# Linear-attention block on one core: the last two token tiles of each slab of keys and values interleaved in two PSUM banks

## The chip, the cores and the metric

The kernel runs on one core of a Trainium2 chip. The metric is the device time of one execution in microseconds (us). Beside the timed runs there is one profiled execution, from which every row below comes; its own time differs a little from that of the timed runs.

## What is computed

One block for 2048 tokens of width 1024, in fp32: layer norm, a linear attention with 32 heads of 32 and a learned feature map, an output projection and residual, and a second layer norm with an MLP of width 3584 and residual.

```python
q, k, v = split(layernorm(x) @ wqkv)            # 32 heads of 32
pk = einsum("bhsd,hdf->bhsf", k, w_phi)         # the same for q
phi_k = concat([softmax(pk), softmax(-pk)])     # 64 features a head
kv = einsum("bhsf,bhsd->bhfd", phi_k, v)        # sums over all tokens
z  = einsum("bhsf->bhf", phi_k)
o  = (phi_q @ kv) / (phi_q @ z + 1e-6)
h  = x + o @ wo
out = h + relu(layernorm(h) @ w1) @ w2
```

## The kernel before

**Work and its order.** The 2048 tokens are 16 tiles of 128. They are worked on in two halves, hf = 0 (tiles 0 to 7) and hf = 1 (tiles 8 to 15). In each half come four slabs of keys and values, s = 0 to 3 (8 heads each: 256 columns of keys, with w_phi folded in, and 256 of values), then two slabs of queries. "Slab (1,2)" below is hf = 1, s = 2. Within a slab the tiles follow each other. Every engine works through its instructions strictly in the order in which the program issues them, and that order is written by hand: TensorE's work is a list of items (`item`), each of 8 steps, and other work is hung on steps of that list (`when(step, ...)`, `do(item, k, ...)`).

**Products.** A product in fp32 is made of three fast ones: each operand is split into a high and a low part, and a step issues high x high, high x low and low x high (L204, L205, L206), each 128 x 512 columns. A tile of a slab takes 8 steps, one for each weight unit k = 0 to 7, and adds up in one PSUM bank named `mm` (four banks in turn). Tile 0 (or 8), the first of a slab, uses `sum3` (L195, L196, L199), where the product with the low half of a unit comes three steps late.

**Weight units.** A unit is 128 x 512 of weights. A DMA brings it into a ring of six raw tiles; ScalarE copies the high half (L126), and VectorE or GpSimd subtracts for the low half (L130) into a ring of ten places (`RW = 10`). A place falls free after the last step that uses its unit, and then the next unit is split (`Units.advance`). The eight units of a slab are used by all its eight tiles, so two places hold units of the next slab ahead, and the other six are split as the old ones fall free.

**Softmax of a key tile.** `kv_first` runs at the end of the tile's last step: ScalarE copies the values out (L452), VectorE takes maximum and minimum and subtracts them (L455, L456, L458, L459). Then the schedule hangs three stages on the steps behind item n of the tile: the exponential on ScalarE (`kv_exp`, L463), sums, reciprocal and product to phi on VectorE (`kv_second`, L468, L469, L471, tile `kphi`), and the sum z on GpSimd (`kv_z`, L479). For each group of four tiles `kv_third` then issues 64 short matmuls on TensorE, 16 a tile, from phi and the values (L490):

```python
for (hf, s, t), n in kv_n.items():
    when(8 * n + 11, kv_exp, (hf, s, t))
    when(8 * n + 13, kv_second, (hf, s, t))
    when(8 * n + 18, kv_z, (hf, s, t))
    when(8 * (n + (3 - t % 4)) + 22, kv_third, (hf, s, t))
```

For a query tile `q_first` (L550, L551, L555, L556) stands in the place of `kv_first`.

**Other work at the same time.** In the second half GpSimd also multiplies exponentials of queries by z, 128 x 1024 (`xl`, L614), VectorE reduces them (`xtz`, L618), GpSimd makes the denominators (`qden`, L652, L653) and VectorE their reciprocals (`smx`, L622). GpSimd further makes sums of MLP weights (L388, tiles `b` and `xn`).

Of the kernel before, what the change touches and what calls it, by code (L numbers as in the profile page):

```python
# [23 lines left out]
HT = NT // 2  # L24
# [117 lines left out]
def kernel(  # L142
# [22 lines left out]
    def mm_bank():  # L165
        return psum.tile([P, 512], F32, name="mm", bufs=4)
# [15 lines left out]
    def woven(ap):  # L182

        return ap.rearrange("p (a b) -> p b a", a=2)

    def unwoven(ps):

        return ps.rearrange("p (b a) -> p a b", a=2)
# [13 lines left out]
    def mm3(ps, a_hi, a_lo, b_hi, b_lo, first, last, more=False):  # L202
        b_hi, b_lo = woven(b_hi), woven(b_lo)
        pe.matmul(ps, a_hi, b_hi, start=first, stop=False, skip_group_check=more)  # L204
        pe.matmul(ps, a_hi, b_lo, start=False, stop=False, skip_group_check=more)  # L205
        pe.matmul(ps, a_lo, b_hi, start=False, stop=last, skip_group_check=more)  # L206
# [4 lines left out]
    def do(n, k, f, *args):  # L211
        at[n, k].append((f, args))
# [232 lines left out]
    xT = {}  # L445
    e_of, v_of, phi_of, kv_ps, kd_of = {}, {}, {}, {}, {}

    def kv_first(key, ps):

        pk = ps.rearrange("p (h f a) -> p a h f", a=2, f=32)[:, 0]  # L450
        vt = kp.tile([P, 256], F32, name="vt", bufs=6)
        act.activation(vt, unwoven(ps)[:, 1], AF.Copy)  # L452
        v_of[key] = vt
        m = kp.tile([P, 2, 8], F32, name="kmx", bufs=2)
        v.tensor_reduce(out=m[:, 0, :], in_=pk, op=ALU.max, axis=AX.X)  # L455
        v.tensor_reduce(out=m[:, 1, :], in_=pk, op=ALU.min, axis=AX.X)  # L456
        e = kp.tile([P, 8, 2, 32], F32, name="ke", bufs=2)
        v.tensor_sub(e[:, :, 0, :], pk, m[:, 0, :, None].to_broadcast([P, 8, 32]))  # L458
        v.tensor_sub(e[:, :, 1, :], m[:, 1, :, None].to_broadcast([P, 8, 32]), pk)  # L459
        e_of[key] = e  # L460
# [62 lines left out]
    def project(t, keys):  # L523
        ps = mm_bank()
        if t in (HT, 0) and keys[0] != ("kv", 0, 0, 0):
            def part(k):
                w = W.get(keys[k])
                return xT[t][:, 0, k, :], xT[t][:, 1, k, :], w[:, 0, :], w[:, 1, :]
            yield from sum3(ps, [partial(part, k) for k in range(NK)], 3)
            return ps  # L530
        for k in range(NK):
            w = W.get(keys[k])
            mm3(ps, xT[t][:, 0, k, :], xT[t][:, 1, k, :], w[:, 0, :], w[:, 1, :], k == 0, k == NK - 1)
            yield
        return ps

    def kv_item(key, keys):
        ps = yield from project(key[2], keys)
        kv_first(key, ps)

    def q_item(s, t, keys):
        ps = yield from project(t, keys)
        q_first(s, t, ps)

    def q_first(s, t, ps):

        pq = ps.rearrange("p (h f w) -> p w h f", w=2, f=32)
        pa = ps.rearrange("p (a c f w) -> p w a c f", w=2, a=2, c=4)
        m = pqp.tile([P, 2, 16], F32, name="qmx", bufs=2)
        v.tensor_reduce(out=m[:, 0, :].rearrange("p (w h) -> p w h", w=2), in_=pq, op=ALU.max, axis=AX.X)  # L550
        v.tensor_reduce(out=m[:, 1, :].rearrange("p (w h) -> p w h", w=2), in_=pq, op=ALU.min, axis=AX.X)  # L551
        e = pqp.tile([P, 4, 2, 4, 32], F32, name="qe", bufs=2)
        m = m.rearrange("p s (w a c) -> p s w a c", w=2, a=2)
        x = e.rearrange("p (w a) s c f -> p s w a c f", w=2)
        v.tensor_sub(x[:, 0], pa, m[:, 0, :, :, :, None].to_broadcast([P, 2, 2, 4, 32]))  # L555
        v.tensor_sub(x[:, 1], m[:, 1, :, :, :, None].to_broadcast([P, 2, 2, 4, 32]), pa)  # L556
        e_of[s, t] = e
# [434 lines left out]
    def item(gen, *args, keys):  # L992
        items.append((gen, args + (keys,)))
        steps.extend((k,) for k in keys)
        return len(items) - 1

    kv_n, q_n, wo_n, up_n, down_n = {}, {}, {}, {}, {}
    for hf in range(2):
        for s in range(4):
            for t in range(hf * HT, (hf + 1) * HT):  # L1000
                kv_n[hf, s, t] = item(kv_item, (hf, s, t), keys=[("kv", hf, s, k) for k in range(NK)])
        for s in range(2):
            for t in range(hf * HT, (hf + 1) * HT):
                q_n[s, t] = item(q_item, s, t, keys=[("q", hf, s, k) for k in range(NK)])

    wo_first = len(items)
    for b, tiles in enumerate(groups):
        for hf in range(2):

            pairs = b == 0 and hf == 0  # L1010
            for j in range(0, 4, 2 if pairs else 1):
# [3 lines left out]
                for half in range(2):  # L1015
                    n = item(wo_pair, tiles[j:j + 2], hf, half, keys=[("wo", hf, 4 * half + k // 2) for k in range(8)])
# [8 lines left out]
    for b in range(2):  # L1025
        for m in DOWN:
            for p in range(NP):
                down_n[b, m, p] = len(items)
                keys = ("a", b, m, p), ("w2", b, m, p)
# [13 lines left out]
    def when(step, f, *args):  # L1043

        if step < 8 * first_up:
            do(step // 8, step % 8, f, *args)
        else:
            do(first_up + (step - 8 * first_up) // 4, step % 4, f, *args)
# [5 lines left out]
    for t in range(1, NT):  # L1054
        n = t - 1 if t < HT else q_n[1, t - HT] + 1
# [32 lines left out]


    for (hf, s, t), n in kv_n.items():  # L1090
        when(8 * n + 11, kv_exp, (hf, s, t))
        when(8 * n + 13, kv_second, (hf, s, t))
        when(8 * n + 18, kv_z, (hf, s, t))
        when(8 * (n + (3 - t % 4)) + 22, kv_third, (hf, s, t))
        if hf == 1 and t == NT - 1:
            do(n + 3, 7, z_sum, s)
            do(n + 3, 7, kv_turn, s)
# [75 lines left out]
    for u in range(32):  # L1173
# [12 lines left out]
        if u in EARLY:  # L1186
            slab, after = EARLY[u]
# [77 lines left out]
    for b in range(2):  # L1265
        for m in DOWN:
            n = down_n[b, m, NP - 1] + 1
# [10 lines left out]
    W = Units(nc, wraw, wring, load, ready, steps)  # L1278
    half = consts.tile([P, 1], F32, name="half")
# [98 lines left out]
```

## Time and profile before

| | |
|---|---|
| time, median of 3 runs | 1791.92 us (1791.12 to 1792.53) |
| profiled execution, its own time | 1796.31 us |
| its span, first to last instruction | 1794.3 us |
| mean granted TensorE clock | 0.996 of full speed |
| busy: TensorE / VectorE / ScalarE / GpSimd | 1771.9 / 1075.9 / 770.1 / 980.2 us |
| matmuls | 10088 |

Busy time is the time in which an engine has an instruction running. A granted clock of 1.00 is the full speed of TensorE, 0.50 half of it.

### The profile page before, as it was taken

What the parts mean: (1) busy time and instruction counts of PE and PEld (TensorE: products, weight loads), DVE (VectorE), ACT (ScalarE), POOL (GpSimd) and SP (SyncE); (2) the same over time, 40 slices, a digit from 0 to 9 for tenths busy, and PEclk for the clock granted to TensorE, in tenths of its full rate; (3) what the DMA queues carried; (4) which work ended last, traced back from release to release, by engine and by line L of the source; (5) the groups of instructions that cost most, each with busy time, mean ns of one, the idle gap of its engine ahead of it and who ended that gap; (6) DMA issues with size and microseconds to landing.
All of it is one profiled execution on the core that took longest, in us unless ns stands there. A gap on an engine that the chain in (4) does not pass through costs nothing.

```text
span 1794.3 us, 28978 instructions
## 1 busy us (share of the span) xinstructions
PE 1771.9 (99%) x10088; PEld 1527.4 (85%) x10088; DVE 1075.9 (60%) x1647; ACT 770.1 (43%) x1379; POOL 980.2 (55%) x991
## 2 busy tenths in 40 slices
PE   9999999999999999999999999999999999999998
PEld 7888888888888877888888888888888888888887
DVE  7888789777789877564766673444434333443333
ACT  5322245233333333355555554444444444444442
POOL 4888755898847987342333224432354544544543
PEclk9999999999999999999999999999999999999999
DMA  6989799665477776887889987777677777877775
GB/s 224 294 289 319 257 286 290 204 191 173 156 226 215 234 228 212 286 266 225 267 267 266 350 286 230 252 248 228 217 245 227 219 240 240 260 227 228 226 227 175
DMA packets 335747, 435.14 MB, mean 243 GB/s; under 512 B 29808, under 2 KB 195696, under 8 KB 335600
## 3 DMA queue, kind: packets, MB, share of 16 engines
q1 hardware_dynamic: 301808, 416.51, 73.3%
q10 hardware_dynamic: 33792, 16.78, 3.3%
q8 instruction: 79, 1.29, 0.3%
q14 instruction: 68, 0.56, 0.1%
HBM read 295.31 MB, written 137.89 MB: 241 GB/s over the span
## 4 chain that ended last, share of the span: by engine, by line
PE 78%; POOL 9%; DVE 5%; DMA 4%; issue 2%; ACT 1%; SPq 0%; ACTq 0%; POOLq 0%; DVEq 0%
PE mm L204 18%; PE mm L205 18%; PE mm L206 18%; PE ac L206 4%; PE ac L204 4%; PE ac L205 4%; PE tp L204 2%; PE tp L206 2%; PE tp L205 2%; POOL b L388 2%; POOL w L130 2%; POOL xl L614 1%; PE mm L199 1%; PE mm L195 1%; POOL zacc L479 1%
## 5 line engine op out<-in xcount | busy, mean ns | idle before, releaser
L130 POOL TENSOR_TENSOR w<-raw,w 128x512 fp32r<-128x512 f32 x357 | 475.5, 1334 | 626.1 <-ACT w L126 599.9
L126 ACT ACTIVATE w<-raw 128x512 fp32r<-128x512 f32 x686 | 410.3, 625 | 468.4 <-PE mm L206 200.7
L130 DVE TENSOR_TENSOR w<-raw,w 128x512 fp32r<-128x512 f32 x329 | 274.3, 835 | 467.4 <-ACT w L126 456.5
L204 PE MATMUL mm<-w,xT 128*128 128x512 f32 x680 | 262.2, 386 | 0.0
L205 PE MATMUL mm<-w,xT 128*128 128x512 f32 x680 | 257.9, 379 | 0.6 <-POOL w L426 0.6
L206 PE MATMUL mm<-w,xT 128*128 128x512 f32 x680 | 257.8, 379 | 0.0
L204 PE MATMUL mm<-hT,w 128*128 128x512 f32 x624 | 236.5, 379 | 0.0
L205 PE MATMUL mm<-hT,w 128*128 128x512 f32 x624 | 236.5, 379 | 0.0
L206 PE MATMUL mm<-hT,w 128*128 128x512 f32 x624 | 236.5, 379 | 0.0
L388 POOL TENSOR_TENSOR b<-b 128x256 f32<-128x256 f32 x164 | 133.8, 816 | 52.2 <-DMA b<-in_w_dram 41.1
L204 PE MATMUL mm<-w 128*128 128x512 f32 x392 | 148.6, 379 | 0.0
L205 PE MATMUL mm<-w 128*128 128x512 f32 x392 | 148.6, 379 | 0.0
L206 PE MATMUL mm<-w 128*128 128x512 f32 x392 | 148.6, 379 | 0.0
L204 PEld LDWEIGHTS mm<-w,xT 128*128 128x128 f32 x680 | 128.5, 189 | 21.6 <-issue 3.3
L206 PEld LDWEIGHTS mm<-w,xT 128*128 128x128 f32 x680 | 128.5, 189 | 18.4 <-DVE xT L180 0.3
L205 PEld LDWEIGHTS mm<-w,xT 128*128 128x128 f32 x680 | 128.6, 189 | 18.1 <-POOL w L426 1.2
L204 PEld LDWEIGHTS mm<-hT,w 128*128 128x128 f32 x624 | 117.9, 189 | 16.8
L206 PEld LDWEIGHTS mm<-hT,w 128*128 128x128 f32 x624 | 117.9, 189 | 16.7
L205 PEld LDWEIGHTS mm<-hT,w 128*128 128x128 f32 x624 | 117.9, 189 | 16.7
L463 ACT ACTIVATE ke<-ke 128x512 f32<-128x512 f32 x64 | 40.3, 629 | 105.4 <-DVE ke L459 105.3
L205 PEld LDWEIGHTS mm<-w 128*128 128x128 f32 x392 | 74.1, 189 | 10.5
L206 PEld LDWEIGHTS mm<-w 128*128 128x128 f32 x392 | 74.1, 189 | 10.5
(192 smaller groups left out, 3359.8 us busy)
## 6 DMA issues: line engine op xcount, KB each, us to landing
raw<-t SPq DMA_DIRECT2D x224, 256.0 KB, 4.0
raw<-ad SPq DMA_DIRECT2D x196, 256.0 KB, 3.1
raw<-in_w_dram SPq DMA_DIRECT2D x168, 256.0 KB, 3.4
ad<-c SPq DMA_DIRECT2D x112, 256.0 KB, 4.0
ad<-s SPq DMA_DIRECT2D x84, 256.0 KB, 4.8
b<-in_w_dram SPq DMA_DIRECT2D x41, 512.0 KB, 6.3
t<-b SPq DMA_DIRECT2D x41, 512.0 KB, 4.7
ed<-qe ACTq DMA_DIRECT2D x64, 256.0 KB, 3.8
```

The source lines that it names most:

```text
L126: nc.scalar.activation(w[:, 0, :], raw[1], AF.Copy)
L130: eng.tensor_tensor(out=w[:, 1, :], in0=raw[1], in1=w[:, 0, :].bitcast(F32), op=ALU.subtract)
L195: pe.matmul(ps, a_hi, woven(b_hi), start=first and k == 0, stop=False, skip_group_check=more)
L199: pe.matmul(ps, a_hi, woven(b_lo), start=False, stop=last and j == n - 1, skip_group_check=more)
L204: pe.matmul(ps, a_hi, b_hi, start=first, stop=False, skip_group_check=more)
L205: pe.matmul(ps, a_hi, b_lo, start=False, stop=False, skip_group_check=more)
L206: pe.matmul(ps, a_lo, b_hi, start=False, stop=last, skip_group_check=more)
L388: pool.tensor_tensor(out=tsum[*u, *out], in0=tsum[*u, *a], in1=tsum[*u, *b], op=ALU.subtract)
L463: act.activation(e_of[key], e_of[key], AF.Exp)
L479: pool.tensor_tensor(out=zacc[s], in0=zacc[s], in1=phi_of[key], op=ALU.add)
L614: pool.tensor_tensor(out=e, in0=e, in1=zb[:, q, None, P * r:P * (r + 1)].to_broadcast([P, 8, P]), op=ALU.mult)
```

## The change

For every slab of keys and values but (0,0), the last two tiles, called A and B here (6 and 7, or 14 and 15), are one pair in two items: in each item four units are used, each for A and then for B, in two banks. The number of items and steps stays the same. `kv_first` of A is issued one step before the pair's end, that of B at its end. Both tiles now count from the second item; the stages of B behind `kv_first` come three steps later than those of A, and `kv_third` stays where it was. Below the new function, lines of the program move down by 17, so L614, L618, L622, L550 are L631, L635, L639, L567 in the changed kernel.

```diff
--- before.py
+++ after.py
@@ -537,6 +537,23 @@
     def kv_item(key, keys):
         ps = yield from project(key[2], keys)
         kv_first(key, ps)
+
+    pair_ps = {}
+
+    def kv_pair(hf, s, tiles, half, keys):
+
+        if half == 0:
+            for t in tiles:
+                pair_ps[t] = mm_bank()
+        for k in range(8):
+            c, t = 4 * half + k // 2, tiles[k % 2]
+            w = W.get(keys[k])
+            mm3(pair_ps[t], xT[t][:, 0, c, :], xT[t][:, 1, c, :], w[:, 0, :], w[:, 1, :], c == 0, c == 7)
+            yield
+            if c == 7 and k < 7:
+                kv_first((hf, s, t), pair_ps.pop(t))
+        if half == 1:
+            kv_first((hf, s, t), pair_ps.pop(t))
 
     def q_item(s, t, keys):
         ps = yield from project(t, keys)
@@ -997,8 +1014,14 @@
     kv_n, q_n, wo_n, up_n, down_n = {}, {}, {}, {}, {}
     for hf in range(2):
         for s in range(4):
-            for t in range(hf * HT, (hf + 1) * HT):
+            last = 0 if hf == s == 0 else 2
+            for t in range(hf * HT, (hf + 1) * HT - last):
                 kv_n[hf, s, t] = item(kv_item, (hf, s, t), keys=[("kv", hf, s, k) for k in range(NK)])
+            if last:
+                two = (hf + 1) * HT - 2, (hf + 1) * HT - 1
+                for half in range(2):
+                    n = item(kv_pair, hf, s, two, half, keys=[("kv", hf, s, 4 * half + k // 2) for k in range(8)])
+                kv_n[hf, s, two[0]] = kv_n[hf, s, two[1]] = n
         for s in range(2):
             for t in range(hf * HT, (hf + 1) * HT):
                 q_n[s, t] = item(q_item, s, t, keys=[("q", hf, s, k) for k in range(NK)])
@@ -1088,10 +1111,11 @@
 
 
     for (hf, s, t), n in kv_n.items():
-        when(8 * n + 11, kv_exp, (hf, s, t))
-        when(8 * n + 13, kv_second, (hf, s, t))
-        when(8 * n + 18, kv_z, (hf, s, t))
-        when(8 * (n + (3 - t % 4)) + 22, kv_third, (hf, s, t))
+        after = 3 if t % HT == HT - 1 and (hf, s) != (0, 0) else 0
+        when(8 * n + after + 11, kv_exp, (hf, s, t))
+        when(8 * n + after + 13, kv_second, (hf, s, t))
+        when(8 * n + after + 18, kv_z, (hf, s, t))
+        when(8 * kv_n[hf, s, t | 3] + 22, kv_third, (hf, s, t))
         if hf == 1 and t == NT - 1:
             do(n + 3, 7, z_sum, s)
             do(n + 3, 7, kv_turn, s)
```

TensorE at the end of slab (1,1), its last six rows before; `w` are units, `xT` the tiles of tokens (3842 is A, 3934 is B), `mm` the banks:

```order
L204 MATMUL mm_4839<-w_4368,xT_3934 128x512
L205 MATMUL mm_4839<-w_4368,xT_3934 128x512
L206 MATMUL mm_4839<-w_4368,xT_3934 128x512
L204 MATMUL mm_4839<-w_4383,xT_3934 128x512
L205 MATMUL mm_4839<-w_4383,xT_3934 128x512
L206 MATMUL mm_4839<-w_4383,xT_3934 128x512
```

The same place after:

```order
L204 MATMUL mm_4785<-w_4365,xT_3842 128x512
L205 MATMUL mm_4785<-w_4365,xT_3842 128x512
L206 MATMUL mm_4785<-w_4365,xT_3842 128x512
L204 MATMUL mm_4786<-w_4365,xT_3934 128x512
L205 MATMUL mm_4786<-w_4365,xT_3934 128x512
L206 MATMUL mm_4786<-w_4365,xT_3934 128x512
```

Two steps used two units, and use one unit now, in two banks.

GpSimd ahead of the end of slab (1,2), before; `zacc` is the sum z, the splits are L130:

```order
L614 TENSOR_TENSOR xl_5252<-xl_5252,zb_2981 128x1024
L388 TENSOR_TENSOR xn_5225<-xn_5225 128x256 x3
L130 TENSOR_TENSOR w_5367<-raw_4869,w_5367 128x512
L388 TENSOR_TENSOR xn_5225<-xn_5225 128x256
L479 TENSOR_TENSOR zacc2_362<-zacc2_362,kphi_5344 128x512
L130 TENSOR_TENSOR w_5387<-raw_4896,w_5387 128x512
L130 TENSOR_TENSOR w_5410<-raw_4964,w_5410 128x512
L652 TENSOR_TENSOR qden_5404<-qden_5404,smx_2984 128x32
```

And after:

```order
L130 TENSOR_TENSOR w_5327<-raw_4857,w_5327 128x512
L479 TENSOR_TENSOR zacc2_362<-zacc2_362,kphi_5266 128x512
L631 TENSOR_TENSOR xl_5252<-xl_5252,zb_2975 128x1024
L388 TENSOR_TENSOR xn_5225<-xn_5225 128x256 x4
L130 TENSOR_TENSOR w_5375<-raw_4878,w_5375 128x512
L479 TENSOR_TENSOR zacc2_362<-zacc2_362,kphi_5350 128x512
L130 TENSOR_TENSOR w_5392<-raw_4930,w_5392 128x512
L669 TENSOR_TENSOR qden_5400<-qden_5400,smx_2978 128x32
```

The first of the three splits has moved ahead of the product `xl`.

VectorE at the end of slab (1,1), before. `ke_4927` belongs to B, `mm_4930` is the bank of T0, the first tile of the next slab:

```order
L618 TENSOR_REDUCE xtz_4946<-xl_4823 128x32
L468 TENSOR_REDUCE ksm_4951<-ke_4927 128x16
L469 RECIPROCAL ksm_4951<-ksm_4951 128x16
L471 TENSOR_TENSOR kphi_4954<-ke_4927,ksm_4951 128x512
L455 TENSOR_REDUCE kmx_4980<-mm_4930 128x8
L456 TENSOR_REDUCE kmx_4980<-mm_4930 128x8
L458 TENSOR_TENSOR ke_4983<-mm_4930,kmx_4980 128x8x32
L459 TENSOR_TENSOR ke_4983<-kmx_4980,mm_4930 128x8x32
```

After, `ke_4907` is A's, `ke_4921` B's and `mm_4924` the bank of T0:

```order
L635 TENSOR_REDUCE xtz_4945<-xl_4836 128x32
L130 TENSOR_TENSOR w_4947<-raw_4830,w_4947 128x512
L468 TENSOR_REDUCE ksm_4956<-ke_4907 128x16
L469 RECIPROCAL ksm_4956<-ksm_4956 128x16
L471 TENSOR_TENSOR kphi_4959<-ke_4907,ksm_4956 128x512
L455 TENSOR_REDUCE kmx_4980<-mm_4924 128x8
L456 TENSOR_REDUCE kmx_4980<-mm_4924 128x8
L458 TENSOR_TENSOR ke_4983<-mm_4924,kmx_4980 128x8x32
L459 TENSOR_TENSOR ke_4983<-kmx_4980,mm_4924 128x8x32
L468 TENSOR_REDUCE ksm_4990<-ke_4921 128x16
L469 RECIPROCAL ksm_4990<-ksm_4990 128x16
L471 TENSOR_TENSOR kphi_4993<-ke_4921,ksm_4990 128x512
```

Where B's three instructions stood, A's stand, behind a split; B's have moved behind the four of T0. At the end of (1,3) it is the same, with the four instructions of the first query tile (L567, L568, L572, L573) between A's and B's, and no split ahead of A's; at the end of (1,2) as at (1,1), with the reciprocal `smx` and no `xtz` ahead of the split.

## Rows read from the trace of the kernel before

**Rows 1.** The page: busy us of the engines, share of the span, instructions.
```profile
PE 1771.9 (99%) x10088; PEld 1527.4 (85%) x10088; DVE 1075.9 (60%) x1647; ACT 770.1 (43%) x1379; POOL 980.2 (55%) x991
```

**Rows 2.** Waits of TensorE: waited for, us in total, times, longest us.
```profile
PE tp L268 <- ACT xin L261: 4.3, 1, 4.3
PE mm L199 <- POOL w L130: 3.7, 5, 1.0
...
PE ac L685 <- DVE qe L672: 2.2, 1, 2.2
```

**Rows 3.** TensorE timeline: start, us, instruction, [idle before, releaser]; behind (1,1), (1,2).
```profile
392.72 0.70 PE L199 MATMUL mm<-w,xT 128*128 128x512 f32 x2 [0.65 <-POOL w L130]
394.39 0.70 PE L199 MATMUL mm<-w,xT 128*128 128x512 f32 x2 [0.97 <-POOL w L130]
...
440.24 0.70 PE L199 MATMUL mm<-w,xT 128*128 128x512 f32 x2 [1.02 <-POOL w L130]
441.46 0.70 PE L199 MATMUL mm<-w,xT 128*128 128x512 f32 x2 [0.52 <-POOL w L130]
```

**Rows 4.** TensorE timeline: L490 behind (1,0), (1,1), (1,2) and (1,3).
```profile
352.57 1.10 PE L490 MATMUL ac<-kphi,vt 128*32 128x64 f32 x64
...
399.56 1.26 PE L490 MATMUL ac<-kphi,vt 128*32 128x64 f32 x64
...
446.63 1.10 PE L490 MATMUL ac<-kphi,vt 128*32 128x64 f32 x64
...
492.51 0.43 PE L490 MATMUL ac<-kphi,vt 128*32 128x64 f32 x16 [0.16 <-DVE kphi L471]
```

**Rows 5.** VectorE timeline, end of slab (1,1).
```profile
397.25 1.22 DVE L618 TENSOR_REDUCE xtz<-xl 128x32 f32<-128x1024 f32 x1 [1.98 <-POOL xl L614]
398.38 0.68 DVE L468 TENSOR_REDUCE ksm<-ke 128x16 f32<-128x512 f32 x1
...
399.38 0.85 DVE L471 TENSOR_TENSOR kphi<-ke,ksm 128x512 f32<-128x512 f32 x1
400.16 0.41 DVE L455 TENSOR_REDUCE kmx<-mm 128x8 f32<-128x256 f32 x1
...
401.48 0.72 DVE L130 TENSOR_TENSOR w<-raw,w 128x512 fp32r<-128x512 f32 x1
```

**Rows 6.** VectorE timeline, end of slab (1,3).
```profile
490.51 0.68 DVE L468 TENSOR_REDUCE ksm<-ke 128x16 f32<-128x512 f32 x1
...
491.50 0.86 DVE L471 TENSOR_TENSOR kphi<-ke,ksm 128x512 f32<-128x512 f32 x1
492.28 0.68 DVE L550 TENSOR_REDUCE qmx<-mm 128x16 f32<-128x512 f32 x1
...
494.67 0.34 DVE L622 RECIPROCAL smx<-qden 128x32 f32<-128x32 f32 x1
```

**Rows 7.** VectorE timeline, end of slab (1,2).
```profile
441.99 0.35 DVE L622 RECIPROCAL smx<-qden 128x32 f32<-128x32 f32 x1 [2.84 <-POOL qden L653]
...
443.20 1.77 DVE L471 TENSOR_TENSOR kphi<-ke,ksm 128x512 f32<-128x512 f32 x1
```

**Rows 8.** GpSimd timeline, end of slab (1,2).
```profile
429.42 2.38 POOL L614 TENSOR_TENSOR xl<-xl,zb 128x1024 f32<-128x1024 f32 x1 [2.33 <-DMA xl<-ed]
...
438.93 2.48 POOL L130 TENSOR_TENSOR w<-raw,w 128x512 fp32r<-128x512 f32 x2
```

**Rows 9.** VectorE timeline, end of slab (1,0).
```profile
349.06 0.41 DVE L455 TENSOR_REDUCE kmx<-mm 128x8 f32<-128x256 f32 x1
```

**Rows 10.** Windows: length, busy us of PE, PEld, DVE, ACT, POOL, PEclk, DMA, GB/s.
```profile
668.00:675.00 7.00, 6.93 (x50) 4.96 (x50) 3.42 (x5) 3.25 (x8) 6.53 (x9) 0.56 0.19 43
701.00:705.00 4.00, 4.00 (x28) 2.97 (x13) 3.34 (x6) 2.61 (x7) 4.00 (x3) 0.57 0.58 195
500.00:520.00 20.00, 20.00 (x94) 17.53 (x93) 16.47 (x25) 6.11 (x8) 4.95 (x8) 1.00 0.74 231
429.40:441.40 12.00, 10.52 (x48) 8.56 (x46) 8.66 (x15) 6.79 (x15) 11.83 (x10) 1.00 0.07 24
```

## The prediction

> **What bounds the kernel now.** I read the waits of TensorE first, then its timeline at each end of a slab, then the timelines of VectorE and GpSimd at the same places, and last the granted clock around the long idles. TensorE is the bound: the page gives it 1771.9 us busy of a span of 1794.3 [rows 1]. So a change can only give back idle time of TensorE, or add some. In the slabs of keys and values there is one kind of idle that this change aims at: the first tile of a slab waits for the low half of a weight unit that GpSimd still has to split, 3.7 us in five waits [rows 2]. They stand behind three of the seven slabs that are paired now: 0.65 and 0.97 us behind slab (1,1), 1.02 and 0.52 us behind (1,2) [rows 3], and the rest of the 3.7, 0.54 us, behind (0,2). That is the most that earlier splits can give back, 0.21% of the time. What can be measured here from no change is about 0.2%, 3.6 us, so even the whole of it would hardly be seen.
>
> The second thing to read is what TensorE takes from VectorE at the same ends: the sums over a group of four tiles (L490) need phi of the slab's last tile, and 64 short matmuls in order stand or fall with the last 16. At the end of (1,1) and (1,3) this phi is ready only as it is wanted. Undelayed, 64 of them take 1.10 us, as behind (1,0) and (1,2); behind (1,1) the row has 1.26, and behind (1,3) the last 16 wait 0.16 us for kphi [rows 4]. In the rows of VectorE the phi of (1,1) ends at 399.38 + 0.85 = 400.23 [rows 5], that of (1,3) at 491.50 + 0.86 = 492.36 [rows 6]. There is no slack there: each us that phi comes later is a us in which TensorE stands.
>
> **The change, part by part.** Matmuls: the same number, with the same operands, in another order. A pair holds two of the four banks named mm at once. The second was last used by a tile whose last matmul lies a whole tile of 24 matmuls back, and VectorE needs it for 1.3 us (four rows such as 400.16 to 401.48 [rows 5]). Cost 0; a bank not drained would show as a wait for L452 or L459 on the first matmuls of a pair.
>
> Units: those of the old slab fall free at every second step of 16 instead of at every step of the last 8, so six splits of the next slab may start up to eight steps earlier. Behind (0,2) and (1,2) GpSimd can use that. Behind (1,2) it idles 2.33 us for a DMA right before L614 at 429.42, and from there to the end of the two splits that TensorE waits for (438.93, 2.48 us) it is busy 11.83 of 12.00 us [rows 8, 10]; the order of after puts one split ahead of that idle, so the two end earlier by one split, half of the 2.48 at least, and of the 1.54 us of waits I let 1.4 go (bounds 1.2 and 1.54). The 0.54 behind (0,2) goes too. Behind (1,1) the same set of GpSimd instructions stands ahead of the last split as before; what is gained or not there doesn't matter, for VectorE is later still (next).
>
> Softmax of the last tiles: this is the costly part. VectorE works in the order written. Before, the three instructions that make the last phi (L468, L469, L471) stood ahead of the softmax start of the next slab's first tile T0. Now A's three stand in that place, then T0's start, and B's three only then, since B's stage comes three steps later. L490 keeps its step.
> At (1,1), up to the reduction that waits for GpSimd's xl the row is as before (397.25, 1.22 us). Then a split stands ahead of A, 0.72 us as the one at 401.48; A's phi ends at 400.23 + 0.72 = 400.95. T0's four instructions take from 400.16 to 401.48, 1.32 us, and B's three as long as the last three before, from 398.38 to 400.16, 1.78 us [rows 5]. So B's phi ends at 400.95 + 1.32 + 1.78 = 404.05 instead of 400.23: 3.8 us later, with no slack before. TensorE coming earlier by a saved wait only waits longer: +3.8 us against before, with no gain. Bounds: 2.5 if contention on VectorE falls, 5 if L471 takes 1.77 us as in [rows 7] instead of 0.85.
> At (1,3) nothing is put ahead of A, which ends at 492.36. Between A and B stand q's four instructions, from 492.28 to 494.67, 2.39 us, and B's three take 490.51 to 492.28, 1.77 us [rows 6]: B's phi comes 4.2 us later, and there was no slack: +4.2 us, bounds 3 to 5.2.
> At (1,2) the last phi ended at 443.20 + 1.77 = 444.97 [rows 7]; L490 started at 446.63, its last quarter some 0.66 us on [rows 4], so phi had 2.3 us. TensorE comes 1.4 us earlier, which leaves 0.9. The new order costs 0.72 + 1.32 + 1.78 = 3.8; the reciprocal ahead of it, late by 2.84 us for GpSimd [rows 7], comes some 1.75 us earlier with GpSimd's work. 3.8 - 1.75 - 0.9 is 1.1; I take +1.0, bounds 0 and 2.
> At the four other ends GpSimd and VectorE have room. The nearest case is (1,0): T0's start was at 349.06 [rows 9], 1.32 + 1.78 behind it is 352.2, and the last quarter of L490 is wanted at 352.57 + 0.66 = 353.2 [rows 4]. Cost 0, with 1.0 us of cover.
>
> What the idles do to TensorE's clock: the kernel before has two long idles further on. An idle of 4.3 us for L261 and one of 2.2 us for L672 [rows 2]. Behind the first, the stretch 668 to 675 has a mean granted clock of 0.56: at half clock most of the time, 1.2 instead of 2.4 GHz, and 7.00 x 0.44 = 3.1 us of work lost. Behind the second, 701 to 705 has 0.57: 4.00 x 0.43 = 1.7 us [rows 10]. The new idles at (1,1) and (1,3), about 4 us each, lie between the two; the one at (1,1) is cut into 0.8 and 3 us by A's 16 short matmuls. I take the middle, 2.4 us each: +4.8, bounds 0 (neither drops) and 6.2 (both as the first). The 1 us at (1,2) is as long as the wait at 440.24, and the stretch with that wait in it has the full clock, 1.00 [rows 3, 10]: 0.
> The Trainium skill, TensorE: Matmul & The Clock Gate, Part 1 (The HAM clock gate), says that the slow clock is the default state and activity releases it, so that an idle costs more than its own length; the trace agrees (0.56 and 0.57 of the clock behind the two idles), and by rows alone of the idle's length the sum below would be 4.8 us less.
>
> **The sum.** -0.5 (0,2), -1.4 (1,2) waits for splits; +3.8, +1.0, +4.2 waits for phi; +4.8 clock: +11.9 us. Does a later stage give it back? From 500 to 520 GpSimd is busy only 4.95 of 20 us [rows 10], waiting for what TensorE and VectorE hand on; its work for the stage after starts from there, and so all that is later moves with TensorE. I count nothing back. The profiled execution took 1796.31 us, 4.4 more than the median of the runs, 1791.92; the sum against it gives 1808.2, against the median **1803.8 us**.
>
> **The rivals.**
> 1. Stalls for phi without the loss of clock: two idles of some 3 to 4 us that end before the clock falls. For it: each is cut by short matmuls at L490. Against it: an idle of 2.2 us was enough once. Sum 11.9 - 4.8 = 7.1: 1799.0, with the smaller bounds (2.5, 0 and 3) 1795.5.
> 2. Faster: the five waits go, and no phi is late. It would need VectorE to reach the last tiles earlier, that is, GpSimd to hand on its qden and xl some 4 us earlier at (1,1) and (1,3). For it: splits are taken from the crowded last eight steps. Against it: the same set of GpSimd work stands ahead of xl there. 1791.9 - 3.7 = 1788.2. It decides at a phi delay of under 1 us at both places.
> 3. No change: GpSimd comes 2 to 3 us earlier there, phi waits of 1 to 2 us in all stand against 1.4 to 3.7 saved, or later waits of TensorE behind 660 (4.3 and 2.2 us [rows 2]) shrink by what was added. 1789 to 1795.
>
> **How the numbers follow.** Stalls with a loss of clock 0.6 (1799 to 1810), stalls without it 0.2 (1795.5 to 1799.5), no change 0.12, faster by 3.6 us or more 0.08. The upper bound of all terms is +5 + 2 + 5.2 + 6.2 - 0.5 = 17.9, 1809.8; the range takes the first two cases whole, 1795 to 1810. Slower by over 0.2% has 0.8, within it 0.12, faster 0.08.
>
> **What would show it.** In the waits of TensorE, L490 for kphi with some 8 to 9 us in all: near 4 at the ends of (1,1) and (1,3), about 1 at (1,2). In the timeline of VectorE at these places T0's (or q's) start between the phi of A and that of B. L199's waits for L130 gone behind (0,2), nearly so behind (1,2). A mean granted clock clearly under 1 in the 4 us behind 404 and behind 497. I am wrong if xl or qden comes earlier from GpSimd, so that B's phi is in time; if B's three instructions stand elsewhere than the order shows; or if the loss comes from a bank not drained at a pair's start.

## The result and the profile after

| | before | changed |
|---|---|---|
| time, median of 6 runs each | 1792.40 us (1791.12 to 1793.62) | 1800.61 us (1799.25 to 1801.46) |
| ratio, 95% interval | | 1.0045 [1.0032, 1.0058] |
| profiled execution / its span | 1796.31 / 1794.3 us | 1801.11 / 1799.1 us |
| TensorE busy | 1771.9 us | 1771.9 us |

The changed kernel is 0.45% slower, 8.2 us, inside the range that was given and 3.2 us under the forecast of 1803.8. In these two profiled executions TensorE's busy time is the same to 0.1 us, so the 4.8 us between their spans are idle time of TensorE; why the timed difference is larger is told under **Nothing given back** below. The view of TensorE's waits in the changed kernel (waited for, us in total, times, longest):

```profile
PE ac L490 <- DVE kphi L471: 7.8, 4, 3.6
PE tp L268 <- ACT xin L261: 4.2, 1, 4.2
...
PE mm L199 <- POOL w L130: 1.4, 3, 0.8
PE ac L702 <- DVE qe L689: 0.8, 1, 0.8
...
PE mm L204 <- DVE ke L459: 0.6, 1, 0.6
```

Against [rows 2]: the waits for splits fell from 3.7 to 1.4 us, which is the gain that the change aimed at, and a wait for kphi that hardly existed rose to 7.8 us. The timeline of TensorE has these waits at their places, splits first, then L490:

```profile
257.08 0.48 PE L199 MATMUL mm<-w,xT 128*128 128x512 f32 x1 [0.25 <-POOL w L130]
...
393.88 0.70 PE L199 MATMUL mm<-w,xT 128*128 128x512 f32 x2 [0.80 <-POOL w L130]
...
400.30 0.43 PE L490 MATMUL ac<-kphi,vt 128*32 128x64 f32 x16 [0.61 <-DVE kphi L471]
403.42 0.43 PE L490 MATMUL ac<-kphi,vt 128*32 128x64 f32 x16 [2.69 <-DVE kphi L471]
...
444.72 0.48 PE L199 MATMUL mm<-w,xT 128*128 128x512 f32 x1 [0.34 <-POOL w L130]
...
451.67 0.43 PE L490 MATMUL ac<-kphi,vt 128*32 128x64 f32 x16 [0.92 <-DVE kphi L471]
...
500.28 0.65 PE L490 MATMUL ac<-kphi,vt 128*32 128x64 f32 x16 [3.56 <-DVE kphi L471]
```

These answer to [rows 3, 4]. At the end of (1,1) A's 16 matmuls wait 0.61 us and B's 2.69; at (1,2) B's wait 0.92; at (1,3) 3.56. The wait behind (0,2) is gone; a small one (0.25, at 257.08) is new in the first tile of the second slab of queries of the first half. VectorE shows why, at (1,1):

```profile
396.73 1.22 DVE L635 TENSOR_REDUCE xtz<-xl 128x32 f32<-128x1024 f32 x1 [1.97 <-POOL xl L631]
397.87 0.68 DVE L130 TENSOR_TENSOR w<-raw,w 128x512 fp32r<-128x512 f32 x1
...
399.46 0.69 DVE L471 TENSOR_TENSOR kphi<-ke,ksm 128x512 f32<-128x512 f32 x1
400.07 0.42 DVE L455 TENSOR_REDUCE kmx<-mm 128x8 f32<-128x256 f32 x1
...
401.40 0.68 DVE L468 TENSOR_REDUCE ksm<-ke 128x16 f32<-128x512 f32 x1
...
402.40 0.88 DVE L471 TENSOR_TENSOR kphi<-ke,ksm 128x512 f32<-128x512 f32 x1
```

The first L471 is A's, the second B's; T0's start (400.07 to 401.40) stands between them, and none of these rows but the first waits for anything: VectorE is busy, in the order written. Counted from the start of xtz, the last phi ends after 402.40 + 0.88 - 396.73 = 6.55 us; before it was 399.38 + 0.85 - 397.25 = 2.98 [rows 5]. At (1,3) the same, with the query's start between:

```profile
493.14 1.22 DVE L635 TENSOR_REDUCE xtz<-xl 128x32 f32<-128x1024 f32 x1 [1.97 <-POOL xl L631]
...
495.28 0.85 DVE L471 TENSOR_TENSOR kphi<-ke,ksm 128x512 f32<-128x512 f32 x1
496.05 0.68 DVE L567 TENSOR_REDUCE qmx<-mm 128x16 f32<-128x512 f32 x1
...
499.44 0.69 DVE L471 TENSOR_TENSOR kphi<-ke,ksm 128x512 f32<-128x512 f32 x1
```

The windows (columns as in [rows 10]) behind the two long idles, and of the stage after 660:

```profile
402.00:409.00 7.00, 5.58 (x32) 4.61 (x33) 6.04 (x16) 1.22 (x3) 6.79 (x8) 0.76 0.30 102
499.00:506.00 7.00, 5.72 (x34) 4.81 (x35) 5.28 (x11) 1.55 (x2) 1.27 (x1) 0.76 0.81 276
669.00:721.00 52.00, 47.00 (x332) 38.18 (x330) 40.95 (x63) 18.63 (x46) 42.84 (x49) 0.97 0.68 220
```

In each of the first two, 7.00 x 0.24 = 1.7 us of work are lost to the clock, as behind the shorter of the two idles of [rows 10].

### The profile page after: what moved, and what is told of

It reads as the page before. It is cut to its first block, busy times and chain, and to the rows that moved or that the text cites. A ratio compares the mean times of both kernels' runs of the same rounds, so it can differ in the third digit from the quotient of the medians.

```text
span 1799.1 us, 28976 instructions
## 1 busy us (share of the span) xinstructions
PE 1771.9 (98%) x10088; PEld 1528.3 (85%) x10088; DVE 1076.3 (60%) x1647; ACT 771.4 (43%) x1379; POOL 979.9 (54%) x991
## 3 DMA queue, kind: packets, MB, share of 16 engines
q8 instruction: 79, 1.29, 0.3%
## 4 chain that ended last, share of the span: by engine, by line
PE 83%; DVE 5%; POOL 4%; DMA 4%; issue 2%; ACT 1%; SPq 0%; ACTq 0%; DVEq 0%; POOLq 0%
PE mm L204 20%; PE mm L205 19%; PE mm L206 19%; PE ac L206 4%; PE ac L204 4%; PE ac L205 4%; PE tp L204 2%; PE tp L206 2%; PE tp L205 2%; POOL w L130 1%; PE mm L196 1%; PE mm L195 1%; PE mm L199 1%; DMA b<-in_w_dram 1%; PE tp L268 1%
## 5 line engine op out<-in xcount | busy, mean ns | idle before, releaser
L130 POOL TENSOR_TENSOR w<-raw,w 128x512 fp32r<-128x512 f32 x357 | 473.2, 1328 | 626.0 <-ACT w L126 572.1
L130 DVE TENSOR_TENSOR w<-raw,w 128x512 fp32r<-128x512 f32 x329 | 273.0, 831 | 470.0 <-ACT w L126 462.7
L479 POOL TENSOR_TENSOR zacc<-zacc,kphi 128x512 f32<-128x512 f32 x60 | 80.1, 1335 | 21.7 <-DVE kphi L471 21.7
```

Source lines behind the costliest of these rows:

```text
L130: eng.tensor_tensor(out=w[:, 1, :], in0=raw[1], in1=w[:, 0, :].bitcast(F32), op=ALU.subtract)
L479: pool.tensor_tensor(out=zacc[s], in0=zacc[s], in1=phi_of[key], op=ALU.add)
```

## The experiments

Each time stands beside runs of the kernel before on the same chip. Their median is 1791.51 us for "L490 later", "Pairs without the delay of B", "The delay alone" and the second profile of before; 1791.83 us for "The same, with the turn later", "Without the pairs at (1,1) and (1,3)", the first version under "The two better parts together" and the added matmuls; 1792.39 us for the two versions with five and with two pairs that end that paragraph.

**Take the wait away: L490 later.** The sums over a group move 6 steps, and nothing else.

```diff
-        when(8 * kv_n[hf, s, t | 3] + 22, kv_third, (hf, s, t))
+        late3_ = 6 if t % HT > 3 and (hf, s) != (0, 0) else 0
+        when(8 * kv_n[hf, s, t | 3] + 22 + late3_, kv_third, (hf, s, t))
```

> The changed kernel with the sums over a group (L490) 6 steps later for the groups that end in a pair, everything else as changed. Theory: the loss is TensorE standing for B's phi, which came 3.3, 0.9 and 3.6 us after L490 wanted it; 6 steps are 6 x 0.648 = 3.9 us, so the waits for kphi go from 7.8 us to under 0.3, and with them the half-clock stretches behind (1,1) and (1,3). The saved waits for splits stay (1.4 us left of 3.7): 1789.5 to 1791.5 us, 9 to 11 less than the changed kernel. Rival, the interleaving itself costs TensorE (two banks in turn, a bank not drained): the time stays near 1800. Rival, the clock falls for another reason: half-clock stretches stay without idles in front.

Measured: 1790.35 us, ratio to before 0.9995 [0.9987, 1.0004]. The whole loss is gone with this one change of the schedule. With it goes the rival that the interleaving itself costs TensorE the 8 us; a cost of its own of up to about 1 us lies inside the interval and is not excluded. Its waits:

```profile
PE mm L199 <- POOL w L130: 2.1, 2, 1.3
...
PE tp L506 <- DVE kd L500: 1.0, 1, 1.0
...
PE tp L515 <- POOL zacc L479: 0.2, 1, 0.2
```

No wait for kphi is left, and with these idles the half-clock stretches behind (1,1) and (1,3) are gone too, as expected (windows, columns as in [rows 10]):

```profile
400.00:412.00 12.00, 11.75 (x120) 9.44 (x119) 10.61 (x25) 4.39 (x10) 10.71 (x12) 1.00 0.58 188
494.00:506.00 12.00, 10.98 (x56) 8.96 (x57) 10.74 (x20) 3.99 (x7) 1.58 (x5) 1.00 0.89 267
```

Two things were missed in the expectation. The waits for splits are 2.1 us, of it 1.31 at the end of (1,2), where the changed kernel waits 0.34. And the turn of kd (L506, transposes on TensorE), which needs the result of L490 and had not been moved, waits 1.0 us.

**The same, with the turn later.** In addition:

```diff
-            do(n + 3, 7, z_sum, s)
-            do(n + 3, 7, kv_turn, s)
+            do(n + 4, 2, z_sum, s)
+            do(n + 4, 2, kv_turn, s)
```

> The changed kernel with L490 of the paired groups 6 steps later, as in the run before, and the turn of kd and the sum of z 3 steps later. Theory: the new waits of that run, 1.0 us for kd and 0.2 us for zacc, go too: no wait of TensorE in the slabs but 2 us for splits: 1788.5 to 1790.5. Rival: the time does not follow such small waits, 1790 to 1792.

Measured: 1789.74 us, ratio 0.9991 [0.9983, 1.0000]. Both new waits are gone and the waits for splits are 2.1 us as before. That is in the range expected, but 0.04% by the ratios from the run without the turn, which no interval here tells apart; the rival, that the time does not follow such small waits, stays possible.

**Pairs without the delay of B.**

```diff
-        after = 3 if t % HT == HT - 1 and (hf, s) != (0, 0) else 0
+        after = 0
```

> The changed kernel with B's stages no longer 3 steps behind A's: on VectorE B's three instructions stand directly behind A's and ahead of the start of T0 or of the first query tile. Theory (order on VectorE): phi of B comes earlier by the start it no longer waits for, 1.3 us at (1,1) and (1,2) and 2.4 us at (1,3): waits for kphi 2.0, 0 and 1.2 us, 3.2 in all instead of 7.8; idles that short may leave the clock up: 1793 to 1797 us. Rival (two tiles end at once and crowd VectorE, the order between them does not matter): waits of 7 to 8 us, near 1800.

Measured: 1792.92 us, ratio 1.0008 [0.9999, 1.0017], just under the range expected. The wait for kphi is 3.5 us (expected 3.2) in place of 7.8:

```profile
398.78 0.43 PE L490 MATMUL ac<-kphi,vt 128*32 128x64 f32 x16 [0.60 <-DVE kphi L471]
400.68 0.43 PE L490 MATMUL ac<-kphi,vt 128*32 128x64 f32 x16 [1.47 <-DVE kphi L471]
...
493.18 0.43 PE L490 MATMUL ac<-kphi,vt 128*32 128x64 f32 x16 [1.47 <-DVE kphi L471]
```

Two tiles that end at once cost 1.47 us for B at each of the two ends, and the 0.6 us for A at (1,1) that the changed kernel has too; the rest was the start that stood between them. No half-clock stretch follows these idles: the windows 400 to 407 and 493 to 500 have a clock of 1.00.

**The delay alone, without pairs.** The kernel before with

```diff
-        when(8 * n + 11, kv_exp, (hf, s, t))
-        when(8 * n + 13, kv_second, (hf, s, t))
-        when(8 * n + 18, kv_z, (hf, s, t))
+        after = 3 if t % HT == HT - 1 and (hf, s) != (0, 0) else 0
+        when(8 * n + after + 11, kv_exp, (hf, s, t))
+        when(8 * n + after + 13, kv_second, (hf, s, t))
+        when(8 * n + after + 18, kv_z, (hf, s, t))
```

> The kernel before, without pairs, with the stages of the last tile of each slab but (0,0) 3 steps later: this part of the change alone. Theory: the last phi comes later by the start that now stands ahead of it, 1.3 us at (1,1) and 2.4 us at (1,3), where there was no slack, 0 at (1,2): waits for kphi 3.5 to 4 us, waits for splits stay at 3.7: 1795.5 to 1798, more if the clock falls. Rival (the delay is hidden, the pairs cost): 1792, as before.

Measured: 1796.23 us, ratio 1.0028 [1.0019, 1.0038]. The delay alone costs over half of what the change costs. The waits for kphi were under-estimated: 2.78 us at (1,1) and 2.38 at (1,3), 5.2 in all. VectorE at (1,1) tells the reason:

```profile
396.16 1.22 DVE L618 TENSOR_REDUCE xtz<-xl 128x32 f32<-128x1024 f32 x1 [1.98 <-POOL xl L614]
398.80 0.42 DVE L455 TENSOR_REDUCE kmx<-mm 128x8 f32<-128x256 f32 x1 [1.42 <-ACT vt L452]
...
400.13 0.68 DVE L468 TENSOR_REDUCE ksm<-ke 128x16 f32<-128x512 f32 x1
...
401.12 0.85 DVE L471 TENSOR_TENSOR kphi<-ke,ksm 128x512 f32<-128x512 f32 x1
```

The start at 398.80 is T0's. It waits 1.42 us: TensorE's last matmul of T0 starts at 398.16 only, ScalarE's copy of T0's values (L452) runs from 398.38 to 398.76, and the row names that copy as what the start waited for. The last tile's three instructions stand behind the start. I had counted the start's own time and not that it can't begin before T0 is done. Of the expected 3.7 us of waits for splits there were 1.2 in this execution (0.53 behind (0,2), 0.70 behind (1,1)), without any pair. None was left at (1,2), where TensorE came late; at (1,1) the wait differs between executions of the same order, as the last two sections of this part show. Counted from the start of xtz, the last phi ends after 401.12 + 0.85 - 396.16 = 5.81 us: 2.8 more than before, against 3.6 more in the changed kernel. The two parts don't add up, since each fills time that the other leaves idle.

**Without the pairs at (1,1) and (1,3).** These two slabs as before, the five other pairs as changed.

```diff
-            last = 0 if hf == s == 0 else 2
+            last = 0 if hf == s == 0 or (hf, s) in ((1, 1), (1, 3)) else 2
...
-        after = 3 if t % HT == HT - 1 and (hf, s) != (0, 0) else 0
+        after = 3 if t % HT == HT - 1 and (hf, s) not in ((0, 0), (1, 1), (1, 3)) else 0
```

> The changed kernel with the slabs (1,1) and (1,3) left as before (no pair, no delay); the five other pairs stay as changed. Theory: the loss sits at these two ends, 3.3 + 3.6 us of waits and both half-clock stretches; what is left is a wait for kphi of 0.5 to 2 us at (1,2): 1790 to 1793.5, within 0.1% of the kernel before. Rival (each pair costs its share): five sevenths of 8 us remain, 1797.

Measured: 1789.36 us, ratio 0.9986 [0.9978, 0.9995]: faster than before, a little more than expected. So all of the net loss sits at the two ends without slack; the rival, that each pair costs its share (1797), is out. What is left:

```profile
PE mm L199 <- POOL w L130: 1.0, 2, 0.6
PE ac L490 <- DVE kphi L471: 0.9, 1, 0.9
```

**The two better parts together, and what each pair is worth.** First pairs and no delay, L490 3 steps later, the turn 3 steps later:

> Pairs as changed, B's stages not 3 steps behind A's, the sums over a group (L490) of the paired groups 3 steps later, and the two steps that use their result (the turn of kd and the sum of z) 3 steps later as well. Theory: the waits for kphi that were left without the delay, at most 1.5 us at a time, lie inside 3 x 0.648 = 1.9 us and go; nothing waits for kd; waits for splits stay at 1.3 to 2.1 us of the 3.7 to 4.0 before. 1788.5 to 1790.5 us if the kernel before shows about 1791.5 beside it, 0.05 to 0.15% faster than before. Rival (the pairs themselves cost something that no wait shows): 1792 or more.

Measured: 1790.98 us, ratio 0.9994 [0.9985, 1.0003]; waits of 2.1 us for splits and 0.3 for kphi. By the ratio that is 0.06% faster, at the lower end of what was expected, and the time lies 0.5 us over the range given; the interval includes no change at all.

Then the five pairs of the run above with L490 of the last group of (1,2) 2 steps later, `paired = 2 if t % HT > 3 and (hf, s) == (1, 2) else 0`:

> Pairs in five slabs, (1,1) and (1,3) left as before, and L490 of the last group of (1,2) 2 steps later. Theory: the 0.9 us of waiting for kphi at (1,2) lies inside 2 x 0.648 = 1.3 us and goes; waits for splits about 1 us of the 3.7 to 4.0 before: 0.1 to 0.25% faster than the kernel before, some 0.5 us under the run without these two steps. Rival: TensorE comes 0.9 us earlier to the next splits and waits there instead; then no difference to that run, 0.14% faster than before.

Measured: 1788.77 us, ratio 0.9976 [0.9966, 0.9985], the fastest version of the study, 0.24% under the kernel before, as expected. Its waits:

```profile
PE mm L199 <- POOL w L130: 0.8, 2, 0.5
...
PE ac L490 <- DVE kphi L471: 0.2, 1, 0.2
```

The wait for kphi went from 0.9 to 0.2 us and no wait for splits came in its place, which speaks against the rival; the times of the two versions don't decide it, since their intervals overlap.

And the same with pairs in (0,2) and (1,2) alone:

> Pairs in (0,2) and (1,2) alone, the two ends at which the trace before shows waits for splits that GpSimd had room to make earlier, L490 of (1,2) 2 steps later. Theory: the pairs at (0,1), (0,3) and (1,0) buy and cost nothing: the same time as with five pairs, within 0.05%, 0.1 to 0.2% faster than before. Rival (those pairs help by moving other work): nearer to the kernel before.

Measured: 1789.81 us, ratio 0.9986 [0.9978, 0.9995], with 1.5 us of waits for splits. By the ratios it is 0.1% behind the version with five pairs, more than the 0.05% expected, so the three pairs that no wait stood behind may be worth something; the two intervals overlap, so this is not decided.

**What the profile of before shows when it is taken again.**

> The kernel before, profiled once more, to see whether the idles behind 660 and the half-clock stretches of 6.8 and 3.4 us there belong to this kernel or to that one execution. Theory: they vary from execution to execution, and the 4.4 us that the changed kernel's profile won back there are not the change's; another profile then shows a span 2 to 4 us shorter. Rival: the same stretches again, and a span of 1794.

Measured: a span of 1792.1 us, one execution of 1794.06. The windows:

```profile
440.00:447.00 7.00, 5.76 (x18) 4.45 (x19) 4.47 (x9) 2.04 (x5) 6.08 (x7) 0.76 0.75 232
668.00:675.00 7.00, 4.88 (x25) 3.87 (x33) 4.57 (x8) 5.00 (x12) 6.76 (x7) 0.76 0.37 103
700.00:706.00 6.00, 5.83 (x48) 4.92 (x49) 4.91 (x9) 4.30 (x10) 5.35 (x7) 1.00 0.79 281
```

Here the clock falls behind (1,2), where 1.7 us are lost; in the stretch behind 668 it loses 1.7 us instead of 3.1 [rows 10], and behind 700 nothing. So the stretches vary between executions of one kernel. Of the twelve profiles of this study, the one first read lost most to the clock between 660 and 720: 5.1 us, the others 1.7 to 3.4.

**Is lateness given back later?** The kernel before with 18 more matmuls on TensorE, in the second query tile of the second half.

```diff
+    def hold():
+        ps = tp_bank()
+        w = W.get(("q", 1, 0, 0))
+        for j in range(18):
+            pe.matmul(ps, xT[NT - 1][:, 0, 0, :], woven(w[:, 0, :]), start=True, stop=True)
+
+    do(last_kv + 2, 4, hold)
```

> The kernel before with 18 matmuls of 512 columns added on TensorE in the middle of the second query tile of the second half, 3.9 us of work whose result nobody reads; TensorE is later by that without an idle. Theory of the prediction (nothing is given back, all later work moves with TensorE): 3.9 us slower, 1795 to 1796. Rival (the idles behind 660 and the clock stretches behind them shrink when TensorE comes later): 0.5 to 2.5 us slower, with a shorter wait for L672's qe.

Measured: 1796.31 us, ratio 1.0020 [1.0008, 1.0033], by the ratio 3.6 us (1.4 to 5.9) for 3.9 us of added work. Most of it arrives at the end; the upper part of the rival's 0.5 to 2.5 is not excluded. The wait for L672's qe was 1.0 us in this execution, but 0.8 in the one above without added work, so that wait says nothing about it. Up to the added matmuls this is the kernel before, and its waits for splits behind (1,1) are one of 0.54 us; in the profile taken again they are 0.22 and 0.97, against 0.65 and 0.97 in [rows 3].

## Why the prediction was right, point by point

**The mechanism** held at each step: B's phi behind T0's start on VectorE, three ends with a wait for kphi and four without, and no bank that costs anything at a pair. Moving L490 alone takes the loss away, and leaving out two pairs does too. That is shown. The 0.6 us for L459 in the waits of after stand at 74.20, in the second tile of slab (0,1), before any pair.

**Waits for phi**, forecast +3.8, +1.0, +4.2 = 9.0 against before: measured 3.3 - 0 (0.61 + 2.69), 0.9, 3.56 - 0.16 = 3.4, in all 7.6. Each term came out 0.1 to 0.8 us too large. From xtz to the last phi the delay at (1,1) is 3.6 us. At (1,3) it is 4.0, counted from the L471 that stands in the old place: 499.44 + 0.69 - 495.28 = 4.85 to the last phi, 0.86 before [rows 6]. Against 3.8 and 4.2 the walk along VectorE was right to 0.2 us. The other 0.3 and 0.6 us lie in when VectorE's chain begins against TensorE, which I did not follow.

**Waits for splits**, forecast -1.9: measured 3.7 - 1.4 = 2.3. At (1,2) I let 1.4 of 1.54 us go; 0.34 is left in the changed kernel, and 0.34 too where (1,1) has no pair and no stall, so this is not TensorE's lateness, and the term was right to 0.2 us. At (1,1) I counted no gain; 0.80 is inside what three executions of the old order show there (1.62, 1.19 and 0.54). In the three runs with all pairs and L490 moved, 1.31, 1.29 and 1.16 us stay at (1,2). GpSimd's timeline shows where they come from: ahead of the two splits stands the product xl, and in these three runs it waits for a DMA (1.74, 0.66 and 0.47 us). The first row is of the first of them, the second of the run without the pairs at (1,1) and (1,3), in which TensorE begins the next slab at nearly the same time:

```profile
428.75 2.37 POOL L631 TENSOR_TENSOR xl<-xl,zb 128x1024 f32<-128x1024 f32 x1 [1.74 <-DMA xl<-ed]
...
426.91 2.82 POOL L631 TENSOR_TENSOR xl<-xl,zb 128x1024 f32<-128x1024 f32 x1
```

The split that TensorE waits for ends 0.9 us later in the first (438.69 against 437.79), and the wait is 1.0 us longer. The sum took the gain at (1,2) from GpSimd's order alone; it holds in the changed kernel, where xl waits for no DMA. Why this DMA lands late in the three runs is open.

**The clock**, forecast +4.8 as 2.4 at each of the two idles: it fell at both, for 1.7 us each, 3.4. This is the term that was mis-sized most. I took the middle between the two stretches of one execution; the longer one didn't come again in that kernel's second profile. The granted clocks of the timed executions bear the 3.4 us out: their mean is 0.9962 over the six of the changed kernel and 0.9981 over the 78 of the kernel before that ran beside the experiments, and 0.0019 x 1795 is 3.4 us. Without the clock the measured terms add up to 5.3 us, 1797.7. By the time alone the prediction's first rival, stalls without a loss of clock (1799.0), lies nearer to 1800.61 than the forecast of 1803.8 does; it is the clock in these rows that decides against it. The Trainium skill, TensorE: Matmul & The Clock Gate, Part 1 (The HAM clock gate), says that the slow clock is the default state and that activity releases it; the trace agrees, with a clock of 0.76 in both windows behind the idles.

**The sum** with measured terms is -2.3 + 7.6 + 3.4 = 8.7; the timed difference is 8.2 (5.7 to 10.4 by the interval).

**Nothing given back.** The two profiles by themselves seem to speak against it. In the changed kernel TensorE comes out of its idle for L261 9.0 us later (677.08 against 668.07), yet the spans differ by 4.8 only. The row of the kernel before for this stage, to be read against 669 to 721 above, shows what was won back:

```profile
660.00:712.00 52.00, 45.52 (x284) 36.76 (x283) 38.35 (x61) 18.82 (x46) 40.86 (x48) 0.90 0.66 210
```

The kernel before lost 5.1 us to the clock there and the changed one 1.7, and its idle for qe was 2.15 us against 0.83. But the second profile of before has 1.7 and 0.75 in the same stage without any change, so this belongs to the one execution. The added matmuls settle the rest for the most part: lateness goes through. The prediction compared the sum with that profile's own 1796.31 and then took the median as base, and the median was the right one.

## What to carry to other kernels

On engines that work in a written order, a stage that is moved by a few steps passes everything that was written between, and begins no earlier than the last thing that it now stands behind: three steps of delay, 1.9 us, cost 2.8 us of waiting at (1,1) by themselves, because the start of the next tile came between and was not ready. Before such a move, look for who waits for the stage's result and how much slack that wait has at each place; two of seven places had none, and they took more than the other five could give. And when a saved wait and a late input lie behind each other on one engine, count the later of the two, not both; the prediction did so at (1,1), and no run tests that step alone.

## What the runs showed of the hardware

The clock of TensorE fell behind idles shorter than those that I had counted as long enough, and stayed up behind longer ones. In the second profile of before it fell behind (1,2), where TensorE stood twice, with 0.7 us of matmuls at 440.71 between:

```profile
440.71 0.70 PE L199 MATMUL mm<-w,xT 128*128 128x512 f32 x2 [1.30 <-POOL w L130]
441.94 0.94 PE L199 MATMUL mm<-w,xT 128*128 128x512 f32 x2 [0.53 <-POOL w L130]
```

With the delay alone it fell behind (1,1) and not behind (1,3), though the idles were nearly alike (the PE timeline, and the windows behind them):

```profile
402.12 0.43 PE L490 MATMUL ac<-kphi,vt 128*32 128x64 f32 x16 [2.78 <-DVE kphi L471]
...
496.30 0.43 PE L490 MATMUL ac<-kphi,vt 128*32 128x64 f32 x16 [2.38 <-DVE kphi L471]
```

```profile
402.00:409.00 7.00, 6.88 (x38) 5.74 (x39) 6.11 (x14) 1.01 (x2) 6.08 (x7) 0.76 0.78 239
496.00:503.00 7.00, 6.70 (x51) 5.48 (x51) 4.87 (x10) 1.06 (x1) 1.68 (x3) 1.00 0.92 306
```

The idle for L689's qe shows it most plainly: of two that differ by 0.02 us, the first (L490 later) is followed by half clock, the second (five pairs, L490 at (1,2) 2 steps later) is not:

```profile
698.41 0.67 PE L702 MATMUL ac<-qe,kvL 64*32 64x256 f32 x16 [2.08 <-DVE qe L689]
...
695.43 0.67 PE L702 MATMUL ac<-qe,kvL 64*32 64x256 f32 x16 [2.10 <-DVE qe L689]
```

```profile
698.00:705.00 7.00, 6.59 (x41) 5.24 (x42) 6.35 (x12) 4.32 (x9) 6.48 (x8) 0.76 0.52 176
695.00:702.00 7.00, 6.57 (x52) 5.55 (x53) 6.33 (x12) 5.27 (x11) 6.53 (x9) 1.00 0.54 189
```

So the length of an idle alone did not decide it in these runs; the idle for L261, 3.7 to 4.5 us, was followed by half clock in all twelve profiles. Where the clock fell it cost 1.7 us, and in two stretches 3.4: behind L261 in the first profile of before, where the window of [rows 10] holds 3.1 of it, and behind L261 in the run without the delay of B, after an idle of 3.81 us:

```profile
668.00:675.00 7.00, 5.74 (x17) 4.46 (x18) 3.71 (x6) 4.45 (x8) 6.92 (x7) 0.52 0.27 78
```

So the middle of 2.4 us that the prediction took for one idle was measured nowhere. What decides between 0, 1.7 and 3.4 us is open.
